# Row statistics on ScalarE instead of VectorE for five chunks of a fused H3 and Mish kernel, with one cast and one load placed later

## The chip, the cores and the metric

The kernel runs on one core of a Trainium2 chip. The metric is the device time of one execution in microseconds (us); a kernel is timed in several runs and their median is given. The engines are TensorE (PE in the profile; PEld is its weight load), VectorE (DVE), ScalarE (ACT), GpSimd (POOL) and SyncE (SP). SyncE only issues DMAs here. Each engine works through its own instructions in order and waits on semaphores for the others.

## The reference, cut to what matters

```python
x  = q                                   # [2048, 448]
xn = (x - mean(x, -1)) / sqrt(var(x, -1) + 1e-5)
# branch A: kv = shortconv4(k, shift_k) * v;  y = longconv(kv, ssm_k) + kv * ssm_D;  A = xn * y
# branch B: h = xn @ w1 + b1;  B = mish(h) @ w2          # w1: 448 x 1792, w2: 1792 x 448
out = x + A + B
```

All inputs are fp32. The variance is that over the 448 columns of a row.

## The kernel before, in words

The 2048 rows are cut into 8 chunks of 256 (two halves jj = 0, 1 of 128 rows), the 1792 hidden columns into 7 pairs of 128. So there are 56 (chunk, pair) steps i, and the program is a list of slots written by hand: slot 2i holds the w1 matmuls of step i (`g1_mm`, L534), slot 2i + 1 its Mish and split (`mish`, L542 and L87, L88) and the w2 matmuls of step i - 2 (`g2_mm`, L566 to L568). `at(slot, ...)` puts work ahead of a slot's own, `after(slot, ...)` behind it. What stands earlier in this list stands earlier in the queue of its engine.

Every fp32 operand of a large matmul is split in two: ScalarE casts it (high part: ach, XH), VectorE subtracts (low part: acl, XL). Mish reads a pair's sums from PSUM and writes tile `a` (two buffers), the cast and the subtraction read it. In slots in which an octet starts (below, odd ones) the split is held back until the octet's products are under way.

Around the 56 steps stands branch A, in three phases. Up to slot 62: the first transforms of the filter (`f1_mm` with key "h") and of kv. For the eight kv groups VectorE forms four taps (L195 to L205) and the product with v (L208); one tap of each is made by GpSimd (`taps_pool`, L188), after a one-element memset on VectorE (L187) that hands over the tile. `f1_mm` (L152) writes the banks pq and pr, `f1_fold` empties them (ScalarE copy L158, two VectorE instructions L162), `f1_out` stores them to DRAM (L173, DMAs issued by ScalarE). The kv transforms stand at slots 24, 29, 34, 39, 44, 50, 55, 59, the filter's last two at 26 and 32. From slot 66, every three slots, an octet: inverse transform of the octet before (`i1_mm`, L296, which writes bank pa among others), transform of this one (`f2_mm`, L241), products on VectorE (`prod`, L278 to L286). From slot 92: the last transform and the gates.

In this middle phase the w1 matmuls use the same banks as the octets, pa above all: Mish must have read a pair's sums before the next octet's matmuls may write there.

The layernorm of chunks 0 to 2 is done row-wise with PE transposes. Chunks 3 to 7 (the change) take another way: a transposed copy of x is loaded (`xT_load`, tile xn with one buffer), the statistics are computed from the row-wise copy Q[c] (tile qt), GpSimd raises variance + eps to the power -1/2 (L437) and stores mean and factor of each row to DRAM (`nt_store`, L464, tile MR). SyncE loads them back as rows spread over all partitions (`nt_row`, L467, into con), VectorE normalises in two instructions per half (`nt_norm`, L473), ScalarE casts and VectorE subtracts (`nt_split`, L480 and L481). `NT_AT`, `NT_SOON` and `NT_HOW` hold the slots of these steps, counted from b = 14(c - 1), plus 1 for chunks 3 and 4. Before the change the statistics go through `drip`, a list from which VectorE work is taken one at a time between other instructions (`dv()`), and what is left is issued at "flush".

Of the kernel before, what the change touches and what calls it, by code (L numbers as in the profile page):

```python
# [7 lines left out]
F32 = mybir.dt.float32  # L8
F32R = mybir.dt.float32r
AF = mybir.ActivationFunctionType  # L10
ALU = mybir.AluOpType
# [3 lines left out]
S, D, F = 2048, 448, 1792  # L15
# [3 lines left out]
CH = 256  # L19
NCHUNK = S // CH  # L20
NO = 8
EPS = 1e-5
# [10 lines left out]
NT = 3  # L33
NT_AT = {"q": -5, "x": -1, "stats": -2, "flush": 0, "row": (4, 8), "norm": (7, 10), "split": (8, 11)}
NT_SOON = dict(NT_AT, row=(4, 5), norm=(4, 7), split=(6, 8))
NT_HOW = {c: NT_SOON for c in (4, 7)}
NT_HOW[6] = dict(NT_AT, row=(4, 10), norm=(8, 11), split=(9, 12))
NT_HOW[3] = dict(NT_SOON, q=-9, stats=-3, flush=-2)
NT_HOW[5] = dict(NT_AT, q=-8, stats=-4, flush=-2)
EVAC_SOON = 2,  # L40
WARM_N = (448, 448, 448)
FILL_N = (224, 112, 96)
# [3 lines left out]
def tile_kernel(ctx: ExitStack, tc, q, qT, k, v, sk, hT, sD, w10, w1, w2, c_fib, c_g, c_gi, c_i2, out):  # L46
    nc = tc.nc
    V = nc.vector

    def pool(name, bufs=1, stack=ctx, **kw):  # L50
        return stack.enter_context(tc.tile_pool(name=name, bufs=bufs, **kw))
# [3 lines left out]
    mp = pool("mlp")  # L55
# [16 lines left out]
    mhalf = cp.tile([128, 2], F32, name="mhalf")  # L72
    b1t = cp.tile([128, NF], F32, name="b1t")
    mv = cp.tile([128, NJ, 2], F32, name="mv")
# [3 lines left out]
    def rs(c):  # L78
        return rstd[:, 2 * c:2 * c + 2] if c < NT else mv[:, 2 * c:2 * c + 2, 1]
# [28 lines left out]
    drip = []  # L108

    def dv(n=1):  # L110
        for _ in range(n):
            if drip:
                drip.pop(0)()
# [4 lines left out]
    def at(slot, fn, *args):  # L118
        plan.setdefault(int(slot), []).append((fn, args))

    def after(slot, fn, *args):
        plan2.setdefault(int(slot), []).append((fn, args))
# [189 lines left out]
    EE, QA, Q = {}, {}, {}  # L312
# [104 lines left out]
    def xn_tile():  # L417
        return mp.tile([128, 4, CH], F32, name="xn", bufs=1)

    def ln_parts(c):  # L420
        st = mp.tile([128, 2, 6], F32, name="bst", bufs=2)
        ve = mp.tile([128, 2], F32, name="ve", bufs=2)
        if c < NT:
            XN[c] = xn = xn_tile().rearrange("p a b -> p (a b)").rearrange("p (j d) -> p j d", j=2)
        eng = nc.gpsimd if 0 < c < NCHUNK - 1 else V

        def stats(jj):
            V.bn_stats(st[:, jj], Q[c][:, jj])

        def aggr(jj):  # L430
            V.bn_aggr(mv[:, 2 * c + jj], st[:, jj])

        def eps(a, b):
            V.tensor_scalar(ve[:, a:b], mv[:, 2 * c + a:2 * c + b, 1], EPS, None, op0=ALU.add)

        def power(a, b):
            nc.gpsimd.tensor_tensor(rs(c)[:, a:b], ve[:, a:b], mhalf[:, a:b], op=ALU.pow)  # L437

        def norm(jj):
            j = 2 * c + jj  # L440
            eng.tensor_scalar(xn[:, jj, :D], Q[c][:, jj], mv[:, j, 0:1], rs(c)[:, jj:jj + 1],
                              op0=ALU.subtract, op1=ALU.mult)

        def tail(a, b, copy=eng.tensor_copy):
            copy(xn[:, a:b, D:], xn[:, a:b, D - 64:D])

        return stats, aggr, eps, power, norm, tail, ve
# [8 lines left out]
        nc.sync.dma_start(XN[c], qT[c])  # L456

    def nt_stats(c):
        stats, aggr, eps, power, norm, tail, ve = ln_parts(c)
        drip.extend([lambda: stats(0), lambda: stats(1), lambda: aggr(0), lambda: aggr(1),  # L460
                     lambda: (eps(0, 2), power(0, 2), nt_store(c))])

    def nt_store(c):
        nc.gpsimd.dma_start(MR[c].rearrange("j (p t) -> p j t", t=2), mv[:, 2 * c:2 * c + 2])  # L464
# [91 lines left out]
    def g2_mm(i, jjs=(0, 1)):  # L556
        c, p = pairs[i]
        ah, al = AHL[i]
        for n in range(2):
            f = 2 * p + n  # L560
            for jj in jjs:
                if f == 0:
                    P2[c, jj] = g2p.tile([128, 512], F32, name="pg2")
                ps = P2[c, jj][:, :D]
                cs = slice(128 * jj, 128 * jj + 128)
                nc.tensor.matmul(ps, ah[:, n, cs], w2h[:, f], start=f == 0, stop=False)  # L566
                nc.tensor.matmul(ps, ah[:, n, cs], w2l[:, f], start=False, stop=False)  # L567
                nc.tensor.matmul(ps, al[:, n, cs], w2h[:, f], start=False, stop=f == NF - 1)  # L568

    def g2_evac(c, jjs=(0, 1)):  # L570
        x = Q[c]
        for jj in jjs:
            V.tensor_add(x[:, jj], P2.pop((c, jj))[:, :D], x[:, jj])
            dv()
            if late(c):
                nc.sync.dma_start(out[:, 2 * c + jj], x[:, jj])
# [4 lines left out]
    def mlp_slot(s):  # L581
# [16 lines left out]
        else:  # L598
# [6 lines left out]
            if 0 <= j < n - 1:  # L605
                g2_mm(j)
                if pairs[j][1] == NP - 1 and pairs[j][0] in EVAC_SOON:
                    g2_evac(pairs[j][0])
# [78 lines left out]
    for c in range(NT, NCHUNK):  # L687
        at_ = NT_HOW.get(c, NT_AT)
        b = 2 * NP * (c - 1) + (1 if c < 5 else 0)
        at(b + at_["q"], ln_load, c)  # L690
        at(b + at_["x"], xT_load, c)
        at(b + at_["stats"], nt_stats, c)
        at(b + at_["flush"], lambda: dv(len(drip)))
        for jj in range(2):
            at(b + at_["row"][jj], nt_row, c, jj)
            after(b + at_["norm"][jj], nt_norm, c, jj)
            after(b + at_["split"][jj], nt_split, c, jj)
# [28 lines left out]
    stats, aggr, eps, power, norm, tail, ve = ln_parts(0)  # L726
# [35 lines left out]
    for s in range(nslots):  # L762
        j = s // 2 - G2_LAG - 1
        if s % 2 == 0 and j >= 0 and pairs[j][1] == NP - 1 and pairs[j][0] not in EVAC_SOON:
            g2_evac(pairs[j][0])
# [81 lines left out]
```

## Time and profile before

| | |
|---|---|
| median of 3 runs | 360.06 us (359.82 to 360.37) |
| the profiled execution | 360.5 us |
| its span, first to last instruction | 358.7 us |
| mean granted TensorE clock | 1.000 |
| busy: PE, PEld, DVE, ACT, POOL | 351.8, 289.8, 288.7, 144.1, 70.4 us |
| idle time before chunk 6's and the other casts L480, all ten | 25.1 us |

How to read the rows of the profile: a group of instructions has its line, engine, operation, out<-in by the names of the tiles, the shapes, the count, then busy time and mean ns of one, then the idle time of the engine before it and who ended it. A row of the timeline has start and length in us, and in brackets the wait before it and its releaser. ACTq is a DMA issued from ScalarE's queue. Matmuls are pipelined, so the length of one is more than the distance to the next.

### The profile page before, as it was taken

Reading aid. Unit: us, or ns where it says so; the run is one execution under the profiler, and the core shown is the slowest. Engines: PE = TensorE matmul, PEld = TensorE weight load, DVE = VectorE, ACT = ScalarE, POOL = GpSimd, SP = SyncE. Lnnn points to the kernel's source line nnn. Section 1 sums busy time; section 2 is a strip of 40 time slices with the busy share of each in tenths; the row PEclk is TensorE's granted clock in tenths of the full one; section 3 lists DMA queues with packets and bytes.
Section 4 is the critical chain, followed back from the end, with each engine's and each line's share of the span. In section 5 each row is a group of like instructions: output and inputs, shape, how many; then the busy total and the mean of one; then the engine's idle time right before and its main releaser. Section 6 shows DMA issues by size and latency. Waiting matters only on the chain.

```text
span 358.7 us, 7459 instructions
## 1 busy us (share of the span) xinstructions
PE 351.8 (98%) x3092; PEld 289.8 (81%) x3092; DVE 288.7 (80%) x399; ACT 144.1 (40%) x258; POOL 70.4 (20%) x78
## 2 busy tenths in 40 slices
PE   8999999999999999999999999999989999999995
PEld 2988888888888989888988558657847699979794
DVE  5999748999999999999439888868986963788941
ACT  3975652344243343333232432234144333354470
POOL 2037002822220240212000130110130116040030
PEclk9999999999999999999999999999999999999999
DMA  7999976949768536765869479879855566989086
GB/s 263 318 388 297 407 291 167 346 118 262 198 172 313 163 107 168 221 162 128 243 200 351 118 285 293 263 237 353 287 186 156 108 170 255 402 334 278 22 116 140
DMA packets 30691, 83.27 MB, mean 232 GB/s; under 512 B 3137, under 2 KB 15810, under 8 KB 30658
## 3 DMA queue, kind: packets, MB, share of 16 engines
q1 hardware_dynamic: 21842, 47.82, 40.0%
q0 software_dynamic: 4928, 22.95, 20.1%
q10 hardware_dynamic: 3888, 12.03, 12.9%
q8 instruction: 24, 0.39, 0.4%
q14 instruction: 9, 0.07, 0.1%
HBM read 54.34 MB, written 28.45 MB: 231 GB/s over the span
## 4 chain that ended last, share of the span: by engine, by line
PE 49%; DVE 4%; ACT 0%; issue 0%; DVEq 0%
PE pg L566 6%; PE pg L568 6%; PE pg L567 6%; PE pa L534 5%; PE pq L534 5%; PE pa L296 3%; PE pr L534 3%; PE pq L241 3%; PE pr L241 2%; PE pp L534 2%; PE pg L534 2%; PE pa L241 1%; PE pp L350 1%; PE pb L534 1%; DVE x L205 1%; PE pq L296 1%
## 5 line engine op out<-in xcount | busy, mean ns | idle before, releaser
L566 PE MATMUL pg<-w2h,ach 128*128 128x448 f32 x224 | 82.3, 367 | 0.0
L568 PE MATMUL pg<-w2h,acl 128*128 128x448 f32 x224 | 81.3, 363 | 0.0
L567 PE MATMUL pg<-w2l,ach 128*128 128x448 f32 x224 | 81.2, 362 | 0.0
L88 DVE TENSOR_TENSOR acl<-a,ach 128x512 fp32r<-128x512 f32 x56 | 38.9, 695 | 31.5 <-ACT ach L87 31.4
L542 ACT ACTIVATE a<-pg,b1t 128x256 f32<-128x256 f32 x66 | 27.9, 473 | 66.3 <-PE pg L534 44.9
L534 PE MATMUL pg<-XH,w1h 128*128 128x256 f32 x264 | 52.6, 283 | 0.0
L566 PEld LDWEIGHTS pg<-w2h,ach 128*128 128x128 f32 x224 | 42.0, 187 | 9.5 <-issue 5.0
L534 PEld LDWEIGHTS pg<-XH,w1h 128*128 128x128 f32 x264 | 41.4, 188 | 6.9 <-issue 5.6
L568 PEld LDWEIGHTS pg<-w2h,acl 128*128 128x128 f32 x224 | 42.1, 188 | 2.6
L567 PEld LDWEIGHTS pg<-w2l,ach 128*128 128x128 f32 x224 | 42.1, 188 | 2.3
L534 PE MATMUL pg<-XL,w1h 128*128 128x256 f32 x264 | 42.9, 277 | 0.0
L162 DVE TENSOR_TENSOR st<-pq,st 128x896 f32<-128x896 f32 x32 | 34.8, 1088 | 4.4 <-ACT st L158 3.9
L534 PEld LDWEIGHTS pg<-XL,w1h 128*128 128x128 f32 x264 | 35.9, 188 | 0.0
L87 ACT CAST ach<-a 128x512 fp32r<-128x512 f32 x56 | 34.8, 621 | 1.7
L534 PE MATMUL pg<-XH,w1l 128*128 128x256 f32 x198 | 33.6, 278 | 0.0
L188 POOL TENSOR_TENSOR x<-kr,skb 128x896 f32<-128x896 f32 x8 | 17.0, 2126 | 70.9 <-PE pr L152 26.3
L534 PEld LDWEIGHTS pg<-XH,w1l 128*128 128x128 f32 x198 | 27.6, 188 | 0.1
L205 DVE TENSOR_TENSOR x<-x 128x896 f32<-128x896 f32 x24 | 26.2, 1092 | 1.6 <-POOL x L188 0.8
L307 POOL DMA_DIRECT2D E<-qe x14 | 8.8, 632 | 94.2 <-ACT qe L250 94.2
L158 ACT COPY st<-pr 128x896 f32<-128x896 f32 x16 | 14.5, 908 | 13.8 <-PE pr L152 12.3
L542 ACT ACTIVATE a<-pa,b1t 128x256 f32<-128x256 f32 x16 | 6.7, 471 | 31.4 <-PE pa L534 31.4
L152 PE MATMUL pq<-x,con 32*64 32x448 f32 x128 | 15.9, 560 | 0.7 <-DVE x L208 0.7
(165 smaller groups left out, 629.6 us busy)
## 6 DMA issues: line engine op xcount, KB each, us to landing
Dkv<-st ACTq DMA_DIRECT2D x16, 448.0 KB, 5.3
ah<-Dh SPq DMA_DIRECT2D x8, 896.0 KB, 7.1
av<-Dkv SPq DMA_DIRECT2D x8, 896.0 KB, 8.8
e<-E POOLq DMA_DIRECT2D x8, 896.0 KB, 7.3
E<-qe POOLq DMA_DIRECT2D x14, 448.0 KB, 6.9
kr<-in_k_dram SPq DMA_DIRECT2D x10, 448.0 KB, 6.6
Dh<-st ACTq DMA_DIRECT2D x10, 448.0 KB, 6.4
x<-in_hT_dram SPq DMA_DIRECT2D x8, 448.0 KB, 6.4
```

What stands on the lines that cost most here:

```text
L87: nc.scalar.copy(h, raw)
L88: V.tensor_sub(l, raw, h)
L152: nc.tensor.matmul(ps[h][64 * jj:64 * jj + 64, b, :D], f1[rg:rg + 32], x[rg:rg + 32, jj], start=True, stop=True, tile_position=(rg, 64 * jj))
L162: f(st[:, n], e, st[:, 1])
L188: nc.gpsimd.tensor_mul(o, KR[g - u // 2], skb[:, u:u + 1].to_broadcast([128, 2, D]))
L205: V.tensor_add(KV[g], KV[g], o)
L241: nc.tensor.matmul(bk(p, r)[32 * t:32 * t + 32, :D], g[rs, t, c], a[rs, t], start=True, stop=True, tile_position=(64 * r, 32 * t))
L534: nc.tensor.matmul(ps[n], l, r, start=all(m[0] != n for m in seq[:n_]), stop=all(m[0] != n for m in seq[n_ + 1:]))
L542: nc.scalar.activation(a[:, n], ps[n], AF.Mish, bias=b1t[:, 2 * p + n:2 * p + n + 1])
L566: nc.tensor.matmul(ps, ah[:, n, cs], w2h[:, f], start=f == 0, stop=False)
L567: nc.tensor.matmul(ps, ah[:, n, cs], w2l[:, f], start=False, stop=False)
L568: nc.tensor.matmul(ps, al[:, n, cs], w2h[:, f], start=False, stop=f == NF - 1)
```

## The change

The statistics of chunks 3 to 7 leave VectorE. ScalarE now makes two passes over each half: a copy whose running sum gives the row's sum, a multiplication by 1/448 for the mean, and a square of (mean - x) whose running sum gives the squared deviations. Both passes write their elements into a scratch tile that takes one of the two buffers of `a`. GpSimd gets one instruction more, which divides by 448 and adds eps, then the power and the store as before. The six ScalarE instructions of a chunk stand together behind slots 27, 41, 53, 70 and 82; "stats" and "flush" are no longer used.

Two more entries change: the second half of chunk 6 is cast behind slot 83 instead of 82, so behind the Mish of step 41, and chunk 7's transposed x is loaded at slot 84 instead of 83. That load now stands on SyncE behind octet 6's gi table and octet 7's g table and ah load.

```diff
-NT_HOW = {c: NT_SOON for c in (4, 7)}
-NT_HOW[6] = dict(NT_AT, row=(4, 10), norm=(8, 11), split=(9, 12))
+NT_HOW = {c: dict(NT_SOON) for c in (4, 7)}
+NT_HOW[6] = dict(NT_AT, row=(4, 10), norm=(8, 11), split=(9, 13))
+NT_HOW[7]["x"] = 0
...
+NT_STATS = {3: 27, 4: 41, 5: 53, 6: 70, 7: 82}
...
     def nt_stats(c):
-        stats, aggr, eps, power, norm, tail, ve = ln_parts(c)
-        drip.extend([lambda: stats(0), lambda: stats(1), lambda: aggr(0), lambda: aggr(1),
-                     lambda: (eps(0, 2), power(0, 2), nt_store(c))])
+        sums = mp.tile([128, 2, 6], F32, name="bst", bufs=2)
+        ve = mp.tile([128, 2], F32, name="ve", bufs=2)
+        skip = mp.tile([128, 2, CH], F32, name="a", bufs=2).rearrange("p a b -> p (a b)")[:, :D]
+        for jj in range(2):
+            x, mean = Q[c][:, jj], mv[:, 2 * c + jj, 0:1]
+            nc.scalar.activation(skip, x, AF.Copy, accum_out=sums[:, jj, 0:1])
+            nc.scalar.mul(mean, sums[:, jj, 0:1], 1.0 / D)
+            nc.scalar.activation(skip, x, AF.Square, bias=mean, scale=-1.0, accum_out=sums[:, jj, 1:2])
+        nc.gpsimd.tensor_scalar(ve, sums[:, :, 1], 1.0 / D, EPS, op0=ALU.mult, op1=ALU.add)
+        nc.gpsimd.tensor_tensor(rs(c), ve, mhalf, op=ALU.pow)
+        nt_store(c)
...
-        at(b + at_["stats"], nt_stats, c)
-        at(b + at_["flush"], lambda: dv(len(drip)))
+        after(NT_STATS[c], nt_stats, c)
```

What moves is shown at three places. The line numbers of the changed kernel are 2 higher than before up to `nt_stats` and 10 higher from `nt_norm` on to `g2_mm`.

First, ScalarE from octet 5 (slot 81) to the start of octet 6 (slot 84). hs and qe are copies out of the octets' banks, ach<-a the casts behind Mish, a<-pa the Mish of step 41, XH<-xn the second half of chunk 6. Before:

```order
L247 COPY hs<-pa 128x448
L87 CAST ach<-a 128x512
L480 CAST XH<-xn 128x4x128
L542 ACTIVATE a<-pa,b1t 128x256 x2
L87 CAST ach<-a 128x512
L247 COPY qe<-pa 128x448
```

Now:

```order
L249 COPY hs<-pa 128x448
L89 CAST ach<-a 128x512
L466 ACTIVATE a,bst<-qt 128x448
L467 ACTIVATE mv<-bst 128x1
L468 ACTIVATE a,bst<-qt,mv 128x448
L466 ACTIVATE a,bst<-qt 128x448
L467 ACTIVATE mv<-bst 128x1
L468 ACTIVATE a,bst<-qt,mv 128x448
L552 ACTIVATE a<-pa,b1t 128x256 x2
L89 CAST ach<-a 128x512
L490 CAST XH<-xn 128x4x128
L249 COPY qe<-pa 128x448
```

Chunk 7's six instructions stand where the cast stood, and the cast stands behind Mish and its own cast.

Second, ScalarE around slot 27, from the stores of the first kv transform (Dkv) and of filter group 6 (Dh) to the next copy out of pr. Before:

```order
L173 DMA Dkv<-st 64x2x896 x2
L173 DMA Dh<-st 64x2x896 x2
L542 ACTIVATE a<-pg_1046,b1t 128x256 x2
L87 CAST ach<-a 128x512
L158 COPY st<-pr 128x896
```

Now:

```order
L175 DMA Dkv<-st 64x2x896 x2
L466 ACTIVATE a,bst<-qt 128x448
L467 ACTIVATE mv<-bst 128x1
L468 ACTIVATE a,bst<-qt,mv 128x448
L466 ACTIVATE a,bst<-qt 128x448
L467 ACTIVATE mv<-bst 128x1
L468 ACTIVATE a,bst<-qt,mv 128x448
L175 DMA Dh<-st 64x2x896 x2
L552 ACTIVATE a<-pg_1049,b1t 128x256 x2
L89 CAST ach<-a 128x512
L160 COPY st<-pr 128x896
```

Chunk 3's six instructions stand between the two pairs of stores, ahead of the Mish of slot 29.

Third, VectorE behind slot 53, from the subtraction of step 26 over the first taps of kv group 7 (L195 to L205) to the memset for its GpSimd tap and the fold of group 6's transform. Before:

```order
L88 TENSOR_TENSOR acl<-a,ach 128x512
L428 BN_STATS bst<-qt 128x6
L195 TENSOR_TENSOR x<-kr,skb 128x896
L428 BN_STATS bst<-qt 128x6
L431 BN_AGGR mv<-bst 128x2 x2
L434 TENSOR_SCALAR ve<-mv 128x2
L198 TENSOR_TENSOR x<-kr,skb 128x448
L200 TENSOR_TENSOR x<-kr,skb 128x448
L205 TENSOR_TENSOR x<-x 128x896
L88 TENSOR_TENSOR acl<-a,ach 128x512
L187 MEMSET x 1x1
L162 TENSOR_TENSOR st<-pq,st 128x896 x2
```

Now:

```order
L90 TENSOR_TENSOR acl<-a,ach 128x512
L197 TENSOR_TENSOR x<-kr,skb 128x896
L200 TENSOR_TENSOR x<-kr,skb 128x448
L202 TENSOR_TENSOR x<-kr,skb 128x448
L207 TENSOR_TENSOR x<-x 128x896
L90 TENSOR_TENSOR acl<-a,ach 128x512
L189 MEMSET x 1x1
L164 TENSOR_TENSOR st<-pq,st 128x896 x2
```

The five statistics rows are gone, and the rest stands in the same order.

## The prediction

> **What bounds the kernel now.** I read the page's busy shares first: they name the engine that the others serve.
>
> ```profile
> PE 351.8 (98%) x3092; PEld 289.8 (81%) x3092; DVE 288.7 (80%) x399; ACT 144.1 (40%) x258; POOL 70.4 (20%) x78
> ```
>
> TensorE (PE) is at work almost all the time. VectorE (DVE), from which the change takes work, is busy 80% but not the bound, so its shorter list is worth nothing in itself. What can be won is the time in which PE stands still. The view of waits for PE lists all of it (in total, times, longest):
>
> ```profile
> PE pa L296 <- ACT a L542: 1.3, 1, 1.3
> PE pg L711 <- DVE wz L707: 1.0, 1, 1.0
> PE pq L152 <- DVE x L208: 0.7, 1, 0.7
> ```
>
> The 1.0 us is the start-up, which the change does not touch. Two stalls remain, 2.0 us together, and both lie where the change works. Next I read the timeline around each. The first, on ScalarE (ACT), VectorE and PE:
>
> ```profile
> 252.01 0.62 ACT L87 CAST ach<-a 128x512 fp32r<-128x512 f32 x1
> 260.45 0.62 ACT L480 CAST XH<-xn 128x512 fp32r<-128x512 f32 x1 [7.82 <-DVE xn L473]
> 260.98 0.83 ACT L542 ACTIVATE a<-pa,b1t 128x256 f32<-128x256 f32 x2
> ```
>
> ```profile
> 258.01 1.08 DVE L286 TENSOR_TENSOR yc<-yc,yd 128x896 f32<-128x896 f32 x1
> 259.01 1.41 DVE L473 TENSOR_TENSOR xn<-xn,con 128x512 f32<-128x512 f32 x2
> ```
>
> ```profile
> 258.04 0.37 PE L566 MATMUL pg<-w2h,ach 128*128 128x448 f32 x1
> ...
> 261.87 0.59 PE L296 MATMUL pa<-ya,gi 32*64 32x448 f32 x2 [1.25 <-ACT a L542]
> ```
>
> ScalarE stands 7.82 us in front of chunk 6's second cast (slot 82), which needs VectorE's normalisation at 259.01. Behind it in ScalarE's order waits the Mish of pair 41, whose sums in bank pa were complete at about 258.1, when PE went on to the w2 matmuls of 258.04. The next matmuls write pa, so PE waits until Mish has emptied it. This is a stall of order: Mish could have run 2.9 us earlier.
>
> The second is the last f1 transform of kv (slot 59), which waits for VectorE's taps. Here are the steps of that chain, on tile x, VectorE and PE:
>
> ```profile
> L187 DVE MEMSET x<- x1: 59/59/59, 162.1 to 162.1; 1x1 f32 x1
> L188 POOL TENSOR_TENSOR x<-kr,skb x1: 2122/2122/2122, 162.2 to 162.2; 128x896 f32<-128x896 f32 x1
> ```
>
> ```profile
> 164.39 1.09 DVE x L205
> ...
> 167.71 1.10 DVE x L208
> 168.86 0.59 PE pq L152 x2
> ```
>
> The memset on VectorE (162.1) lets GpSimd (POOL) form one tap (162.2, 2.12 us); the add at 164.39 needs it; from there VectorE runs without a gap to 168.8. PE could have begun at 168.86 - 0.7 = 168.1.
>
> **The change part by part.** *Off VectorE.* Per chunk two statistics passes, two aggregates and one small add go:
>
> ```profile
> L428 DVE BATCH_NORM_STATS2 bst<-qt x16: 606/620/627, 3.5 to 263.1; 128x6 f32<-128x448 f32 x16
> L431 DVE BATCH_NORM_AGGREGATE mv<-bst x16: 150/172/183, 4.2 to 266.3; 128x2 f32<-128x6 f32 x16
> ```
>
> That is 2 x 0.62 + 2 x 0.17 and about one more 0.17: 1.75 us a chunk.
>
> *Onto ScalarE.* Six instructions a chunk, each waiting for the one before, since they feed each other or share the scratch tile. Nearest rows: a copy and a scaling of 128x448, and a tiny activation:
>
> ```profile
> L247 ACT COPY hs<-pa 128x448 f32<-128x448 f32 x8 | 4.3, 532 | 5.8 <-PE pb L241 5.8
> L370 ACT ACTIVATE q<-q,rstd 128x448 f32<-128x448 f32 x6 | 3.8, 671 | 1.9 <-DVE q L364 1.9
> ```
>
> ```profile
> L713 ACT ACT_TABLE_LOAD  x1: 1283/1283/1283, 0.7 to 0.7; - x1
> L713 ACT ACTIVATE ve<-mhalf x1: 203/203/203, 2.0 to 2.0; 128x2 f32<-128x2 f32 x1
> ```
>
> A copy pass is 0.53 to 0.67, the mean 0.20, the square pass 0.67: 2 x 1.4 to 2 x 1.54, so 2.8 to 3.1 us. No row shows what the running sum costs; its bounds are nothing and one more tiny activation for each of the four passes, 4 x 0.20 = 0.8. The burst is thus 2.8 to 3.9 us. I take 3.3, about the middle, as no row is nearer to either end.
>
> As engine time this is a bad exchange: 3.3 us for 1.75, 5 x 1.55 = 7.8 us over five chunks, and 367.9 if ScalarE were what the kernel waits for. It is busy 40%, and its time counts only where PE waits for it; so each burst is placed below, and the sum goes by that. The Trainium skill, page "ScalarE: Activation LUTs", section "Rules for kernel authors", speaks against such a move: additions and multiplications belong on VectorE, not ScalarE. By that rule the 367.9 would hold.
>
> *Chunk 7's burst (slot 82) and chunk 6's cast.* The burst starts at 252.01 + 0.62 = 252.6 in ScalarE's 7.82 us gap and ends at 255.9, or 256.5 at the dearest, before pair 41's sums are there at 258.1. Mish runs 258.1 to 259.0, its cast to 259.7, and chunk 6's cast from 260.45 as before. What is late next? The matmuls that stood until 261.87 also need yc, done at 258.01 + 1.08 = 259.1. Nothing is later than PE's own 260.5, so the whole 1.3 us goes. Chunk 6's low part follows its cast as now, and the first matmul that reads it comes only after the whole octet that begins at 260.5.
>
> *Chunk 5's burst (slot 53).* ScalarE, ahead of it:
>
> ```profile
> 153.16 1.24 ACTq L173 DMA_DIRECT2D Dkv<-st  x2
> 157.14 0.84 ACT L542 ACTIVATE a<-pg,b1t 128x256 f32<-128x256 f32 x2 [3.36 <-DMA Dkv<-st]
> ```
>
> The burst runs from 154.4 to 157.7 and pushes this Mish by 0.6 us; its cast ends near 159.2. VectorE, 1.75 us lighter just there, comes to the subtraction that uses the cast at about 159.7 and to the memset at 162.1 - 1.75 = 160.3. GpSimd must first turn the sums into a row statistic:
>
> ```profile
> L437 POOL TENSOR_TENSOR mv<-ve,mhalf x5: 712/1084/1106, 85.6 to 266.7; 128x2 f32<-128x2 f32 x5
> L464 POOL DMA_DIRECT2D MR<-mv x5: 750/767/835, 87.0 to 267.7; - x5
> ```
>
> Its new small operation is not in the trace; between nothing and another 1.08. I take the dear end, as its row is the same shape: 157.7 + 2 x 1.08 + 0.77 = 160.6. The tap starts there instead of 162.2, the chain is 1.6 us earlier, and PE, due at 168.1, finds it done at 167.3. The 0.7 us goes with 0.8 to spare (0.2 with a burst of 3.9).
>
> *Chunk 3's burst (slot 27)* is the dangerous one, because two stores now queue behind it, then Mish. ScalarE, VectorE and PE:
>
> ```profile
> 82.26 1.24 ACTq L173 DMA_DIRECT2D Dkv<-st  x2
> 84.61 2.53 ACTq L173 DMA_DIRECT2D Dh<-st  x2
> 87.19 0.84 ACT L542 ACTIVATE a<-pg,b1t 128x256 f32<-128x256 f32 x2 [4.37 <-DMA Dkv<-st]
> ```
>
> ```profile
> 89.24 0.68 DVE L88 TENSOR_TENSOR acl<-a,ach 128x512 fp32r<-128x512 f32 x1
> ...
> 98.34 2.21 DVE L162 TENSOR_TENSOR st<-pq,st 128x896 f32<-128x896 f32 x2
> ```
>
> ```profile
> 100.75 0.59 PE L152 MATMUL pq<-x,con 32*64 32x448 f32 x2
> ```
>
> From 89.24 VectorE works on with hardly a pause until 98.34 + 2.21 = 100.55, and PE takes bank pq at 100.75: 0.2 us of slack. Now the burst starts at 83.5, ends at 86.8, and the two issues (0.62 each; the first can go out when the last pass starts, 0.6 before its end) put Mish at 83.5 + 3.3 - 0.6 + 1.24 = 87.4, and its cast's end at 88.9. VectorE, freed of 1.75, is waiting then and takes its 89.24 step at 89.0. So nothing is lost, but the 1.75 us here is not won either. A burst of 3.9 makes it 89.6 and costs 0.3 - 0.2 = 0.1 us; each further 0.1 costs 0.1.
>
> *Chunks 4 and 6.* The scratch takes one of two a tiles, so the next Mish waits for the subtraction just before it:
>
> ```profile
> 125.39 0.84 ACT L542 ACTIVATE a<-pg,b1t 128x256 f32<-128x256 f32 x2 [3.43 <-PE pg L534]
> ```
>
> ```profile
> 126.55 0.68 DVE L88 TENSOR_TENSOR acl<-a,ach 128x512 fp32r<-128x512 f32 x1
> ```
>
> ```profile
> 208.12 0.84 ACT L542 ACTIVATE a<-pa,b1t 128x256 f32<-128x256 f32 x2 [5.62 <-PE pa L534]
> ```
>
> Chunk 4's Mish moves from 125.39 to about 127.2 (the stores behind the burst go out before that). Its users are the w2 matmuls two pairs on: free. Chunk 6's burst fits into a 5.62 us gap. *Chunk 7's x load* passes two tables and octet 7's load on SyncE; these no longer wait for the cast that frees its tile, and its reader stands four slots further on. Free.
>
> The sum is 1.3 + 0.7 = 2.0 us. The profiled execution took 360.5 (span 358.7, 1.8 around it) and becomes 358.5; it lay 0.4 above the median of 360.06, which becomes 358.1.
>
> **The rivals.** *A long burst.* If the sums cost more than my bound, say a burst of 4.4, Mish at slot 29 comes at 88.5, VectorE is 0.85 late, PE loses 0.65 at 100.75, and at 168.1 the tap chain (sums at 158.8, tap at 161.7) gives 0.5 of the 0.7: a gain of 1.15, so 358.9; with 5.0 the gain is gone (360.0). For it: the sums have no row. Against: it needs more than a whole extra instruction per pass.
>
> *GpSimd stays the taps' brake.* If its two operations and the store take 1.6 us more than I put down, the 0.7 stays: 358.8. Against: each of them is priced at its dearest row.
>
> *Another wait takes the place of the 1.3.* Then only the 0.7 goes: 359.4. Against: every other input of those matmuls is dated above.
>
> *Table switches, the slower side.* If the square is not in the table with Mish, each burst has one load before the first square and one before the next Mish: 2 x 1.28 = 2.6 us, a burst of 5.9. At slot 29 Mish then comes at 90.0, VectorE's step at 91.6, and PE loses 2.2; the tap chain is 0.4 later than before; the 1.3 is still won, as Mish 41 could start at 258.5. Together +1.3: 361.4. The point of decision is a burst of 5.0. The Trainium skill, page "ScalarE: Activation LUTs", section "Table sets: the hidden batching unit", names copies among the functions in every set, but not squares. It gives a switch another 1.4 us for the drain, which no row here shows. Against it: the trace has Mish, copies and casts after one load, and the changed kernel's order holds one load too, ahead of everything.
>
> *ScalarE as the bound*, the 367.9 above: against it stand its gaps of 7.82 and 5.62 us. *No effect*: both stalls are replaced by others of their size, 360.1.
>
> **How the numbers follow.** Chances: the forecast 0.66, long burst 0.14, GpSimd 0.08, another wait 0.05, tables 0.04, ScalarE as the bound 0.01, no effect 0.02. A measurement of this kernel can tell about 0.2% (0.7 us) from no change, so faster means below 359.3: the forecast, GpSimd, three quarters of the long burst (0.10), half of the other wait (0.03): 0.87. Slower is the tables and ScalarE as the bound, 0.05. The rest, 0.08, is the same. The range's low end is 358.1 less 0.24, by which the lowest of the runs lies under their median, and a little of the weight loads' waits: 357.6. Its high end takes in the long burst up to 4.4, GpSimd and most of the other wait: 359.4. About 0.15 is left outside.
>
> **What would show it.** In the profile after: PE's waits list only the start; Mish 41 starts at 258 less what was won before and the cast of chunk 6 follows it; the six instructions take 2.8 to 3.9 us; bank pq at slot 34 is taken without a wait of 0.2 or more. I am wrong if a new row of PE appears there, if a second table load stands in the trace, or if the tap at slot 55 starts no earlier against PE's f1 than now.

## The result and the profile after

The changed kernel takes 357.85 us (median of 6 runs, 357.71 to 357.95) against 359.95 us before (6 runs, 359.69 to 360.37): a ratio of 0.994, 95% interval 0.9927 to 0.9953, so 1.7 to 2.6 us less. The profiled execution took 357.91 us with a span of 356.1 us, at a mean granted clock of 1.000.

The busy shares of the page after:

```profile
PE 350.7 (98%) x3092; PEld 289.1 (81%) x3092; DVE 282.0 (79%) x374; ACT 160.1 (45%) x308; POOL 72.4 (20%) x83
```

ScalarE is 16 us busier than before and VectorE 6.7 less, and the kernel is faster. PE does the same 3092 matmuls. The view of waits for PE has one row left:

```profile
PE pg L720 <- DVE wz L716: 1.0, 1, 1.0
```

That is the start-up wait; the 1.3 and the 0.7 us are gone. The first of them, at octet 6, in the timeline of ScalarE after (start, length, what it waited for):

```profile
251.50 0.57 ACT L466 ACTIVATE a<-qt 128x448 f32<-128x448 f32 x1
...
254.74 0.19 ACT L468 ACTIVATION_READ_ACCUMULATOR a<-qt,mv 128x1 f32 x1
257.28 0.84 ACT L552 ACTIVATE a<-pa,b1t 128x256 f32<-128x256 f32 x2 [2.35 <-PE pa L544]
258.15 0.62 ACT L89 CAST ach<-a 128x512 fp32r<-128x512 f32 x1
259.43 0.62 ACT L490 CAST XH<-xn 128x512 fp32r<-128x512 f32 x1 [0.66 <-DVE xn L483]
```

Chunk 7's burst lies in the gap in which ScalarE stood before and is over 2.35 us ahead of Mish. Mish 41 now waits for PE's sums, not for a cast behind VectorE's work, and chunk 6's cast comes last. PE goes from the w2 matmuls into the inverse transform without a pause:

```profile
259.23 0.36 PE L578 MATMUL pg<-w2h,acl 128*128 128x448 f32 x1
259.52 0.59 PE L298 MATMUL pa<-ya,gi 32*64 32x448 f32 x2
```

The second, at slot 59: GpSimd and VectorE from chunk 5's statistics to kv group 7's last product, and PE.

```profile
157.73 0.23 POOL L469 TENSOR_SCALAR ve<-bst 128x2 f32<-128x2 f32 x1 [9.47 <-ACT a L468]
158.05 1.57 POOL L470 TENSOR_TENSOR mv<-ve,mhalf 128x2 f32<-128x2 f32 x1
159.92 0.79 POOL L474 DMA_DIRECT2D MR<-mv  x1 [0.30 <-POOL mv L470]
160.73 2.14 POOL L190 TENSOR_TENSOR x<-kr,skb 128x896 f32<-128x896 f32 x1
```

```profile
159.68 0.06 DVE L189 MEMSET x<- 1x1 f32 x1
...
162.91 1.09 DVE L207 TENSOR_TENSOR x<-x 128x896 f32<-128x896 f32 x1 [0.84 <-POOL x L190]
...
166.23 1.09 DVE L210 TENSOR_TENSOR x<-x 128x896 f32<-128x896 f32 x1
```

```profile
167.26 0.62 PE L544 MATMUL pg<-XL,w1h 128*128 128x256 f32 x4
167.81 0.59 PE L154 MATMUL pq<-x,con 32*64 32x448 f32 x2
```

The memset comes 2.4 us earlier than before, but GpSimd is still at the statistics and starts the tap only at 160.73; VectorE waits 0.84 us for it. The product is done at 166.23 + 1.09 = 167.32, and the handover takes 0.05 (before, 168.81 to 168.86). PE takes it at 167.81, without a wait: 0.4 us to spare.

**Where the 2.6 us of the two spans lie.** Follow the start of three PE groups. At slot 34 bank pq was taken at 100.75 and is taken at 100.46: 0.29 earlier, and 0.30 already in the w1 matmuls of 79 us, before the first burst. In the thirteen traces of this document, whose work is alike up to there, these matmuls start between 77.79 and 78.45 us, so this is scatter and not the change. At slot 59 it was 168.86 and is 167.81: 0.76 more, the second stall. At octet 6 it was 261.87 and is 259.52: 1.30 more, the first stall. The last 0.25 comes behind that in steps of 0.1 us that I can't put down to anything. The two stalls are 2.06 us; the medians differ by 2.10.

### The profile page after: what moved, and what is told of

Its sections match the earlier page's. It is cut to its first block, busy times and chain, and to the rows that moved or that the text cites. A ratio compares the mean times of both kernels' runs of the same rounds, so it can differ in the third digit from the quotient of the medians.

```text
span 356.1 us, 7495 instructions
## 1 busy us (share of the span) xinstructions
PE 350.7 (98%) x3092; PEld 289.1 (81%) x3092; DVE 282.0 (79%) x374; ACT 160.1 (45%) x308; POOL 72.4 (20%) x83
## 4 chain that ended last, share of the span: by engine, by line
PE 96%; DMA 2%; ACT 1%; SPq 0%; issue 0%; DVE 0%
PE pg L544 23%; PE pg L576 13%; PE pg L578 13%; PE pg L577 13%; PE pa L544 6%; PE pq L544 5%; PE pq L154 4%; PE pa L298 3%; PE pr L544 3%; PE pq L243 3%; PE pr L243 3%; PE pp L544 2%; DMA kr<-in_w_dram 2%; PE pa L243 1%; PE pp L352 1%; PE pb L544 1%
```

## The experiments

Each run stands beside runs of the kernel before on the same chip; these lay between 359.77 and 360.19 us, so kernels are compared by their ratio to it. The changed kernel's is 0.994. Line numbers in the rows differ by a few between the kernels.

**The cast and the load alone**, on the kernel before:

```diff
-NT_HOW = {c: NT_SOON for c in (4, 7)}
-NT_HOW[6] = dict(NT_AT, row=(4, 10), norm=(8, 11), split=(9, 12))
+NT_HOW = {c: dict(NT_SOON) for c in (4, 7)}
+NT_HOW[6] = dict(NT_AT, row=(4, 10), norm=(8, 11), split=(9, 13))
+NT_HOW[7]["x"] = 0
```

> The kernel before with only chunk 6's second cast behind slot 83 and chunk 7's x load at slot 84; all statistics stay on VectorE. Theory A (two independent stalls, each removed by one part of the change): the 1.3 us at octet 6 goes, the 0.7 us at the last kv transform stays, so 1.3 us less than before, about 358.65. Theory B (the gain is the 8.8 us taken off VectorE, shared over the five chunks; the cast's place alone only moves the wait, as its input still comes from VectorE): within 0.3 us of before.

Measured 358.7 us against 359.77, ratio 0.9968 (0.9956 to 0.9979). PE's waits:

```profile
PE pg L712 <- DVE wz L708: 1.0, 1, 1.0
PE pq L153 <- DVE x L209: 0.7, 1, 0.7
```

The 1.3 is gone and the 0.7 is left, as the theory of two separate stalls has it. The octet's stall is won by moving one cast behind one Mish, with no statistics moved at all.

**The statistics alone**, the cast and the load as before:

```diff
-NT_HOW[6] = dict(NT_AT, row=(4, 10), norm=(8, 11), split=(9, 13))
-NT_HOW[7]["x"] = 0
+NT_HOW[6] = dict(NT_AT, row=(4, 10), norm=(8, 11), split=(9, 12))
```

> The changed kernel with chunk 6's cast back behind slot 82 and chunk 7's x load back at slot 83; all statistics on ScalarE. Theory A: only the 0.7 to 0.8 us at the last kv transform is won, about 359.2, and the wait of PE for Mish at octet 6 stands in its profile with about 1.3 us. Theory B: most of the 2.1 us, about 358.0.

Measured 364.43 us, ratio 1.0132 (1.0115 to 1.0149): slower than before, and both theories missed. ScalarE, then PE's longest wait:

```profile
259.33 0.62 ACT L489 CAST XH<-xn 128x512 fp32r<-128x512 f32 x1 [7.82 <-DVE xn L482]
259.86 0.57 ACT L465 ACTIVATE a<-qt 128x448 f32<-128x448 f32 x1
...
263.09 0.19 ACT L467 ACTIVATION_READ_ACCUMULATOR a<-qt,mv 128x1 f32 x1
263.18 0.82 ACT L551 ACTIVATE a<-pa,b1t 128x256 f32<-128x256 f32 x2
```

```profile
PE pa L297 <- ACT a L551: 4.6, 1, 4.6
```

Cast and burst are both put behind slot 82, and in this kernel the cast is issued first. So the burst did not fall into the 7.82 us gap, as I had expected of it, but behind the waiting cast and ahead of Mish: the wait of 1.3 grew by the burst's 3.4. Compared with the changed kernel, the inverse transform starts 264.05 - 259.52 = 4.5 us later. And that is not all; the windows over the wait, the inverse transform and what follows (length, busy time of PE, PEld, DVE, ACT, POOL, then the granted clock):

```profile
259.00:264.05 5.05, 0.41 (x3) 0.04 (x1) 0.99 (x2) 4.53 (x14) 0.59 (x2) 0.95 0.56 189
264.05:267.17 3.12, 3.12 (x33) 0.88 (x33) 0.69 (x1) 0.60 (x1) 1.10 (x2) 0.53 0.06 13
267.17:268.70 1.53, 1.53 (x41) 0.55 (x39) 1.07 (x2) 1.34 (x2) 0.00 (x0) 1.00 0.00 0
```

After the long wait PE runs the inverse transform at a clock of 0.53, and it takes 3.12 us instead of 1.70 (259.5 to 261.2 in the changed kernel). 4.5 + 1.4 = 5.9, and the spans differ by 362.1 - 356.1 = 6.0. This is the profiled execution, with a mean clock of 0.995. The other executions of this kernel took 363.8 to 365.37 us at mean clocks of 0.993 to 0.988, so what the clock costs differs between them; only the one is explained here.

**The statistics alone, chunk 7's burst ahead of the cast**, to tell the burst's cost from its place:

```diff
-NT_STATS = {3: 27, 4: 41, 5: 53, 6: 70, 7: 82}
+NT_STATS = {3: 27, 4: 41, 5: 53, 6: 70, 7: 81}
```

(and the two lines of the kernel above).

> All statistics on ScalarE, chunk 6's cast behind slot 82 and chunk 7's x load at slot 83 as before the change, but chunk 7's burst behind slot 81, so ahead of the waiting cast and not between it and Mish. Theory A mended (the two parts are independent if the burst does not stand between the cast that waits and Mish): the 1.3 us stall at octet 6 stands as before, the 0.7 us goes, 359.1 to 359.4. Rival (a burst in that stretch delays Mish wherever it stands): 362 or more.

Measured 359.45 us against 360.17, ratio 0.9979 (0.997 to 0.9988). PE's waits:

```profile
PE pa L297 <- ACT a L551: 1.2, 1, 1.2
PE pg L719 <- DVE wz L715: 1.0, 1, 1.0
```

The octet's stall is back at its old size and slot 59's is gone. One slot earlier, the same burst is free; so the 3.4 us that it added to the wait were a matter of order, and only 0.7 of the change's 2 us comes from the statistics.

**Chunk 5 alone, with the cast and the load.** The other chunks keep their statistics on VectorE:

```diff
+    def nt_stats_v(c):
+        stats, aggr, eps, power, norm, tail, ve = ln_parts(c)
+        drip.extend([lambda: stats(0), lambda: stats(1), lambda: aggr(0), lambda: aggr(1),
+                     lambda: (eps(0, 2), power(0, 2), nt_store(c))])
...
-        after(NT_STATS[c], nt_stats, c)
+        if c in (5,):
+            after(NT_STATS[c], nt_stats, c)
+        else:
+            at(b + at_["stats"], nt_stats_v, c)
+            at(b + at_["flush"], lambda: dv(len(drip)))
```

> Only chunk 5's statistics on ScalarE, those of chunks 3, 4, 6 and 7 on VectorE as before; cast and x load as in the changed kernel. Theory A: the whole 2.1 us, within 0.3 us of the changed kernel (357.85). Theory B: a fifth of what VectorE's relief gives, so about 0.4 us less than before, 359.5.

Measured 358.02 us against 359.77, ratio 0.9952 (0.994 to 0.9965). PE waits for nothing but the start-up. One chunk of five gives what the whole change gives, as far as these runs can tell: by the ratios 0.4 us are missing, and the intervals overlap.

**All but chunk 5, with the cast and the load:** as above, with

```diff
-        if c in (5,):
+        if c in (3, 4, 6, 7):
```

> Chunks 3, 4, 6 and 7 on ScalarE, chunk 5's statistics on VectorE as before; cast and x load as in the changed kernel. Theory A: 1.3 us less than before, 358.65, with PE's wait for VectorE at the last kv transform between 0.4 and 0.8 us (VectorE may come to it a little earlier through chunk 4). Theory B: four fifths of the gain and more, about 358.2.

Measured 357.98 us, ratio 0.9948 (0.9934 to 0.9961). The theory missed: in the profiled execution there is no wait at slot 59, although chunk 5's statistics stand on VectorE just ahead of the memset, as before. VectorE and PE:

```profile
166.62 1.09 DVE L210 TENSOR_TENSOR x<-x 128x896 f32<-128x896 f32 x1
```

```profile
167.77 0.59 PE L154 MATMUL pq<-x,con 32*64 32x448 f32 x2
```

The product is done at 167.71 and taken at 167.77, with nothing to spare. An earlier chunk's relief had reached this point. Which one, the next two kernels ask.

**Chunks 3, 6 and 7, with the cast and the load:**

```diff
-        if c in (5,):
+        if c in (3, 6, 7):
```

> Statistics of chunks 3, 6 and 7 on ScalarE, of chunks 4 and 5 on VectorE as before; cast and x load as in the changed kernel. Theory: moving chunk 4's statistics alone or chunk 5's alone takes the wait at the last kv transform away, and chunk 3's does not, because VectorE waits for ScalarE's cast behind that burst; so here PE waits again, 0.5 to 0.8 us, and the time is 358.5 to 358.8. Rival (any chunk's relief reaches that transform): 358.0.

Measured 358.59 us against 360.17, ratio 0.9953 (0.994 to 0.9966). PE's waits, and VectorE behind chunk 3's burst:

```profile
PE pg L729 <- DVE wz L725: 1.0, 1, 1.0
PE pq L154 <- DVE x L210: 0.5, 1, 0.5
```

```profile
88.73 0.69 DVE L90 TENSOR_TENSOR acl<-a,ach 128x512 fp32r<-128x512 f32 x1 [1.19 <-ACT ach L89]
```

The wait at slot 59 is back. Most of what chunk 3's burst takes off VectorE, VectorE spends in waiting for the cast that stands behind this burst.

**Chunk 4 alone, with the cast and the load:**

```diff
-        if c in (5,):
+        if c in (4,):
```

> Only chunk 4's statistics on ScalarE, those of chunks 3, 5, 6 and 7 on VectorE; cast and x load as in the changed kernel. Theory: chunk 4's relief alone, carried by VectorE's unbroken queue from slot 41 to slot 59, takes the 0.7 us away: within 0.3 us of the changed kernel, 357.9. Rival (VectorE's earlier work is eaten up by its waits for PE and ScalarE on the way): PE's wait stays, 358.6.

Measured 358.39 us against the same runs, ratio 0.9952 (0.9938 to 0.9966). The median lies nearer to the rival's 358.6 than to the theory's 357.9, and the intervals of this kernel and the one above cover each other: the times decide nothing. The rows of the profiled executions do. Here PE waits only at the start-up. The product at slot 59 starts at 166.69, and PE takes it at 167.84 with nothing to spare, much as in the kernel with all but chunk 5.

How much of each chunk's relief reaches the chain of slot 59 is read from its memset on VectorE (L187 before), counted from the start of the w1 matmuls near 78 us, which takes the scatter of the start out:

| statistics on ScalarE | memset, us after the w1 matmuls | earlier by |
|---|---|---|
| none (the cast and the load alone) | 161.64 - 78.03 = 83.61 | |
| chunks 3, 6, 7 | 161.50 - 78.02 = 83.48 | 0.13 |
| chunk 4 | 161.05 - 78.15 = 82.90 | 0.71 |
| chunks 3, 4, 6, 7 | 160.99 - 78.08 = 82.91 | 0.70 |
| chunk 5 | 159.93 - 77.79 = 82.14 | 1.47 |
| all five | 159.68 - 78.16 = 81.52 | 2.09 |

Chunk 4's 0.71 is just the 0.7 that is needed. The queue that carries it is not unbroken, as the theory had it: at 142.49 VectorE waits 0.78 us for ScalarE's cast, which it did not do before, and loses there about half of the relief. The rival was right that such waits eat up relief, and wrong about the amount.

**Longer bursts.** Three kernels make one half's group of a burst once more, which changes no result; the timeline has it at 1.73 us. In chunk 3's:

```diff
-        for jj in range(2):
+        for jj in (0, 1, 1) if c == 3 else (0, 1):
```

> The changed kernel with one half of chunk 3's six instructions made twice (9 instructions, 1.73 us more of ScalarE before the Dh stores and the Mish of slot 29). If the prediction's reading of slot 27 holds (0.2 to 0.35 us of slack at the f1 matmuls of slot 34, every further 0.1 us of burst costing 0.1): 1.4 us more than the changed kernel, 359.2, with a new wait of PE for VectorE's st at slot 34. Rival (ScalarE at 45% hides any of this): no difference.

Measured 359.61 us against 360.19, ratio 0.9986 (0.9977 to 0.9995): nearly the whole gain is lost. PE's waits, VectorE, PE:

```profile
PE pg L576 <- DVE qt L583: 1.1, 1, 1.1
PE pg L720 <- DVE wz L716: 1.0, 1, 1.0
```

```profile
90.55 0.69 DVE L90 TENSOR_TENSOR acl<-a,ach 128x512 fp32r<-128x512 f32 x1 [2.92 <-ACT ach L89]
...
99.56 2.20 DVE L164 TENSOR_TENSOR st<-pq,st 128x896 f32<-128x896 f32 x2
```

```profile
99.16 0.47 PE L576 MATMUL pg<-w2h,ach 128*128 128x448 f32 x1 [1.08 <-DVE qt L583]
...
101.82 0.59 PE L154 MATMUL pq<-x,con 32*64 32x448 f32 x2
```

VectorE waits for the cast until 90.55 and is 1.66 us late from there on. PE meets this first one block ahead of where I had looked: the w2 matmuls of slot 33 wait for VectorE to empty the sums before them. Then comes bank pq, taken at 101.82, 1.36 us later than the 100.46 of the changed kernel.

In chunk 7's (`c == 7`):

> The same 1.73 us more of ScalarE, in chunk 7's burst at slot 82. ScalarE still stands 2.35 us behind that burst, until the sums of step 41 are there, so the first theory says no difference to the changed kernel (within 0.3 us). Rival (ScalarE's added time costs at any place what it costs at slot 27): 1.4 us more.

Measured 357.98 us, ratio 0.9943 (0.9929 to 0.9957), and PE waits only at the start-up. The same 1.73 us of ScalarE's time cost nothing here.

In chunk 5's (`c == 5`):

> The same 1.73 us more of ScalarE, in chunk 5's burst at slot 53. GpSimd's tap, which waits for the burst's sums through its own two operations and the store, starts 1.7 us later, and the last kv transform has about 0.4 us to spare: 1.3 us more than the changed kernel, 359.15, with PE's wait for VectorE there again. Rival (the tap is bound by the memset on VectorE alone): up to 0.6 us more.

Measured 358.31 us, ratio 0.9952 (0.994 to 0.9965): 0.4 us more than the changed kernel, and the intervals overlap. PE's waits without that of the start-up, GpSimd, VectorE:

```profile
PE pq L154 <- DMA x<-in_hT_dram: 0.6, 1, 0.6
PE pq L154 <- DVE x L210: 0.3, 1, 0.3
```

```profile
159.59 0.19 POOL L469 TENSOR_SCALAR ve<-bst 128x2 f32<-128x2 f32 x1 [11.20 <-ACT a L468]
159.86 0.72 POOL L470 TENSOR_TENSOR mv<-ve,mhalf 128x2 f32<-128x2 f32 x1
...
161.69 2.15 POOL L190 TENSOR_TENSOR x<-kr,skb 128x896 f32<-128x896 f32 x1
```

```profile
160.90 0.69 DVE L90 TENSOR_TENSOR acl<-a,ach 128x512 fp32r<-128x512 f32 x1 [1.73 <-ACT ach L89]
...
163.87 1.09 DVE L207 TENSOR_TENSOR x<-x 128x896 f32<-128x896 f32 x1
```

The 0.6 is a load at 8.3 us, long before the burst. The expected wait is there, but smaller. The sums reach GpSimd 1.86 us later, yet its power took 0.72 us where it had taken 1.57 (the last section says why), and the tap starts only 161.69 - 160.73 = 0.96 later; less the 0.4 to spare, that is 0.5, of which the view of waits shows 0.3. VectorE came late as well. It stood 1.73 us for the cast behind the longer burst, and the add that needs the tap starts at 163.87 without a wait, just as the tap ends (161.69 + 2.15 = 163.84). So this run does not separate the path through the sums, which I had expected, from the one through the cast, and its time fits the rival's 0.6 as well.

**Chunk 7's x loaded at slot 83 again:**

```diff
-NT_HOW[7]["x"] = 0
```

> The changed kernel with chunk 7's x load back at slot 83, ahead of octet 6's gi and octet 7's g and ah loads; these three then wait on SyncE until chunk 6's low part is formed, as before the change. First theory: they are needed 10 us later or more, no difference to the changed kernel (within 0.3 us). Rival (the load's place is a part of the gain): 0.3 to 1 us more.

Measured 358.21 us, ratio 0.9945 (0.9933 to 0.9957): no difference that this can tell. The load's move is free, and it is worth nothing that these runs can show.

No run beats the changed kernel. In it PE waits for nothing behind the start-up, so a further gain would have to come from PE's own 350.7 us.

## Why the prediction was right, point by point

*The sum of two stalls* held: 1.3 + 0.7 forecast, 1.30 + 0.76 in the rows, 358.1 forecast and 357.85 measured. The kernel with the cast alone and the one with chunk 7's burst ahead take the two terms apart.

*The burst* was put at 3.3 us, between 2.8 and 3.9. Chunk 3's runs from 83.29 to 86.72, 3.43 us. By form, after (count, then busy us and mean ns of one):

```profile
L468 ACT ACTIVATE a<-qt,mv 128x448 f32<-128x448 f32 x10 | 6.7, 671 | 0.3
L466 ACT ACTIVATE a<-qt 128x448 f32<-128x448 f32 x10 | 5.8, 578 | 1.7 <-DVE x L207 0.8 <-DVE st L164 0.8
L467 ACT ACTIVATE mv<-bst 128x1 f32<-128x1 f32 x10 | 2.0, 203 | 0.3
L466 ACT ACTIVATION_READ_ACCUMULATOR a<-qt 128x1 f32 x10 | 1.9, 187 | 0.0
L468 ACT ACTIVATION_READ_ACCUMULATOR a<-qt,mv 128x1 f32 x10 | 1.9, 186 | 0.0
...
L722 ACT ACT_TABLE_LOAD x1 | 1.3, 1283 | 0.7 <-PEq L844 0.7
```

The running sum, which had no row before, is an instruction of its own, 0.19 us, close to the tiny activation that I had set as its dear bound; it starts some 0.1 us before its pass ends, so that four of them add less than 0.8. That takes away the long burst (4.4). One table load stands in the whole trace, so the square brought no switch, and the slower rival falls. The Trainium skill, page "ScalarE: Activation LUTs", section "Rules for kernel authors", would keep such work on VectorE. As a rule on engine time the trace bears it out (16 us more on one engine, 6.7 less on the other). The prediction also took it as a rule on this kernel's time, which gave 367.9; the measurement decides against that reading.

*Chunk 7's burst and chunk 6's cast.* The prediction had the burst fit because the gap is there, and put the stall's end down to the cast's move. Both are right, but it costed the two as if they were separate. They are not: behind slot 82 the burst is free only because the cast has left the place ahead of it. Without that move PE waits 4.64 us instead of 1.25, and loses 1.4 more by the clock. The text should have asked in which order the two stand when both are put behind slot 82.

*Chunk 5's burst* does what was said: the tap starts at 160.73 and PE's input is ready at 167.32, against 160.6 and 167.3 forecast. But PE came 0.3 earlier than in the profile before, with the start-up, and the chain did not, so 0.4 us are to spare instead of 0.8. GpSimd's two small operations took 1.9 us (157.73 to 159.62) instead of the 2.16 reckoned; the burst was a little longer, and the 0.30 us between the power and its store were missing from the sum. The step that failed is the one that gave this 0.7 to chunk 5 alone. The runs with all but chunk 5 and with chunk 4 alone have no wait there either; chunk 4's relief was entered as free, and it is worth the same 0.7. Only one of the two is needed, so the sum does not change; that a path which was not reckoned with covered the same 0.7 is luck. The relief itself was put too high: with chunk 5 alone the memset comes 1.47 us earlier, not 1.75. The prediction added up the lengths of the five instructions, but VectorE starts the next before one ends: the 0.62 us statistics pass of 156.78 in the trace before is followed at 157.31. VectorE's busy time shows the same: 6.7 us less over five chunks, not 8.75.

*Chunk 3's burst* as the dangerous one: 87.4 was forecast for Mish and 89.0 for VectorE's step; they came at 87.37 and 88.89. Bank pq is ready at 97.90 + 2.21 + 0.05 = 100.2 and taken at 100.46, so the slack was 0.3 against the 0.2 forecast:

```profile
87.37 0.84 ACT L552 ACTIVATE a<-pg,b1t 128x256 f32<-128x256 f32 x2 [0.65 <-PE pr L154]
```

```profile
88.89 0.69 DVE L90 TENSOR_TENSOR acl<-a,ach 128x512 fp32r<-128x512 f32 x1 [1.23 <-ACT ach L89]
...
97.90 2.21 DVE L164 TENSOR_TENSOR st<-pq,st 128x896 f32<-128x896 f32 x2
```

That each further 0.1 costs 0.1 fits the one longer burst that was run, 1.36 us on PE for 1.73 with 0.3 of slack, even though the first wait appears a block earlier than named. That next to nothing is won here is shown by VectorE's 1.23 us, and by the 0.13 that reaches slot 59.

*Chunks 4 and 6, the load.* Chunk 4's Mish came at 125.65, not at 127.2. VectorE's subtraction from the tile of the Mish before ran from 126.15 to 126.83, so the new Mish did not write that tile, as the prediction had it. With two tiles in turn it can only have taken the scratch, which was free when the burst ended. Ahead of it stood only the issue of the two stores, until 125.54. Neither that nor chunk 6's burst has a row in PE's waits; the load's move was tried by itself and is free.

## What to carry to other kernels

Ask of a move not how much time it takes on which engine, but what stands between a waiting instruction and the one that frees the bottleneck's buffer: the same 1.7 us on ScalarE cost 1.4 us of PE's time at slot 27 and nothing at slot 82, and the same burst added 3.4 us to a wait or nothing, depending on whether it stood behind the cast or ahead of it. Two edits that stand in one queue must be costed together, in the order in which they will stand. And once a stall is gone, further relief of the same chain buys nothing: one chunk of five did the work of all. Relief is worth what reaches the place that PE waits for: of the statistics of chunks 3, 4 and 5 that was 0.1, 0.7 and 1.5 us.

## What the runs showed of the hardware

A wait of PE can cost more than its length. In the statistics-only kernel PE stood 4.64 us, from 259.41 on. The granted clock was still 1.00 up to 263.5, fell to 0.50 at about 263.6, 4.2 us into the wait, and was back at 1.00 at about 267.0, 3.4 us later and 3.0 us after PE had begun to work again; this cost 1.4 us more. After the 1.3 us wait of the kernel before and the 1.2 us of the kernel with the burst ahead, the inverse transform ran at 1.00 in its usual 1.7 us. The Trainium skill has this rule, page "TensorE: Matmul & The Clock Gate", section "What's actually happening": after an idle window of about 3.4 us the clock falls to half, and about 3.4 us of work bring it back. The trace agrees as to the half and roughly as to the times; how short a wait may be to cause it, between 1.3 and 4.2 us, no run here shows.

A power of 128x2 on GpSimd is no fixed price: between 0.71 and 1.58 us in these traces, with the same shape. What VectorE does when it starts goes with it. For chunk 5 it started at 158.05 in the changed kernel and took 1.57 us, beside this addition on VectorE:

```profile
157.95 1.09 DVE L207 TENSOR_TENSOR x<-x 128x896 f32<-128x896 f32 x1
```

The power ended at 159.62, 0.58 us after this addition (159.04). In the kernel with the longer burst it started at 159.86, while VectorE stood until 160.90, and took 0.72. All 104 powers of 128x2 in the thirteen traces fit this. The 34 that start while VectorE is in a TENSOR_TENSOR with both inputs in SBUF take 0.98 to 1.58 us and end 0.56 to 0.59 us after that instruction. The other 70, with VectorE idle or reading from a PSUM bank, take 0.71 to 0.73. No run was made to test this alone, but no row speaks against it. By it, the 1.08 that the prediction took as the dear end is 0.71 and a wait for VectorE. At slot 59 the wait cost 1.57 - 0.72 = 0.85 us of the spare time, more than the stall of 0.7 was long.
